# Weight conversions of the first block in halves, and some copies moved between ScalarE and VectorE

## The chip, the cores and the metric

The kernel runs on one NeuronCore of a Trainium2 chip. Its metric is the device time of one execution in microseconds (us). The core has five engines that run in parallel, each through its own list of instructions in order: TensorE (PE, matrix products into PSUM), VectorE (DVE), ScalarE (ACT), GpSimd (POOL) and SyncE (SP, which here only issues transfers). An instruction waits on semaphores until what it reads is written and what it overwrites is no longer needed; whatever stands behind it on the same engine waits with it.

## What is computed

The reference, cut to what matters:

```python
# x: (8, 3008, 256), filt_r and filt_i: (1505, 256), w_in: (256, 2048), w_out: (2048, 256)
X = np.fft.rfft(x, axis=1)
Y = X * (filt_r + 1j * filt_i)[None, :, :]
y = np.fft.irfft(Y, n=3008, axis=1).astype(np.float32)

t = y.reshape(8 * 3008, 256)
h = t @ w_in
g = h * np.clip(h + 3.0, 0.0, 6.0) / 6.0
out = g @ w_out                          # float32
```

First a filter along the sequence in the frequency domain, for each of 8 batches; then a two-layer network with a hard swish on each of the 24064 tokens. The two weight matrices come in as 64-bit floats (their scale factor makes them so), which the kernel reads as pairs of 32-bit words and converts itself.

## The kernel before

**Tiling.** The tokens are cut into 47 blocks of 512. A block takes 8 steps (`NP`), one for each 256 columns of the hidden layer: an up-projection (two products of 512 columns in `al` and `be` of PSUM), the hard swish, and in the next step the down-projection, which accumulates in `po`. Blocks from 1 on do this with seven products in place of eight (Strassen's scheme, `up_1` to `up_5`, `g_sums`, `down`), with sums of weight tiles that GpSimd makes once (`w_sums`, L296). Block 0 does it plainly (`plain_up` L653, `plain_down` L662), because the sums don't exist yet.

**The filter.** The Fourier transforms are matrix products in two stages over 3008 = 47 x 64. For batch 0 they run ahead of block 0: `a0_unit` (L348) does the first stage, four products for each half of the channels, and evicts each bank of PSUM with `copy`, on VectorE or ScalarE (L344, L346); `turn` transposes; `b_unit`, `f_unit` and `y_unit` do the second stage and the product with the filter; `bi_unit` and `direct`/`n_first` the way back. Small dummy products (`keep_warm`, L778) are put between. For batches 1 to 7 the same work is spread over the steps of the blocks before they are needed. Of batch 1, `a_unit` (L378) runs once in each of steps 2 to 9, its eight parts `c` in order; both halves of its result are evicted on ScalarE (L388) and stored to DRAM by `z_store`. Later batches evict one half there, and `a_sums` (L392) forms sum and difference on VectorE.

**The weights.** They are 16 parts, part 2p being the 256 columns of the first matrix that step p needs and part 2p + 1 the 256 rows of the second. `w_load` brings a part into a buffer that is borrowed from another pool (`W_AT` names which; a new load waits until the part before the last in the same pool is converted, `w_before`). `w_abs` (L263) makes the absolute value of the high words on ScalarE. `w_conv` (L269) then does the conversion with seven VectorE instructions, L275 to L293; without `w_abs` there is an eighth, L284. The space of `w_all` that the last parts fill holds batch 0's x before.

**Order.** Nothing reorders the work: instructions go to each engine as the Python code emits them. Ahead of block 0 the code is written out (L741 to L830): loads on SP in order, part 0 loaded after the third piece of x, part 1 after the fourth; a conversion after `a0_unit(4)` and after `a0_unit(16)`; parts 2 and 3 converted after the second stage, by `convert(2)` at L830. From then on a plan says what is added to each step: `at(step, fn, ...)`. Functions in `EARLY` (L732) are emitted between up- and down-projection, others at the end of the step. In block 0, step p emits `plain_up(p)`, the early part, `plain_down(p - 1)`, the late part. `plain_up` also emits the two rectifiers on ScalarE (`relu`, L616) and the two gate products on VectorE (`hswish`, L621), which release `al` and `be`. Twelve conversions stand in the late part of steps 0 to 6:

```python
for i, s in enumerate((0, 1, 1, 2, 2, 3, 3, 4, 4, 5, 5, 6)):
    at(s, convert_one)
```

`convert_one` emits `w_abs`, `w_conv` and then whatever loads have their buffer free. The GpSimd sums for weight part i follow from step 6 on, parts 14 and 15 first.

The functions that the change touches, with the line numbers of the profile:

Of the kernel before, what the change touches and what calls it, by code (L numbers as in the profile page):

```python
# [36 lines left out]
HC = NC // 2  # L37
XC = 4
NB = HC // XC
# [6 lines left out]
NP = DFF // 256  # L46
# [90 lines left out]
def kernel(  # L137
# [9 lines left out]
    nc = tc.nc  # L147
# [47 lines left out]
    st = {}  # L195
# [38 lines left out]
    def w_part(i):  # L234
        p = i // 2
        if i % 2 == 0:
            cols = ts(p, 256)
            src = moe_w_in[:, cols].bitcast(I32)
            return src.rearrange("(a p) d -> p a d", p=P), w_in[p][:, 0:4, :].rearrange("p (a j) m -> p a (j m)", a=2)
        src = moe_w_out[ts(p, 2 * P), :].bitcast(I32)  # L240
        return src.rearrange("(a p) d -> p a d", p=P), w_out[p][:, 0:4, :].rearrange("p (a j) m -> p a (j m)", a=2)
# [21 lines left out]
    def w_abs(i):  # L263
        words = st["bits", i].rearrange("p (n two) -> p n two", two=2)
        st["high", i] = sp.tile([P, 512], FP32, name="s1")
        nc.scalar.activation(out=st["high", i], in_=words[:, :, 1].bitcast(FP32), func=AXT.Abs)


    def w_conv(i):  # L269
        words = st.pop(("bits", i)).rearrange("p (n two) -> p n two", two=2)  # L270
        lo, hi = words[:, :, 0], words[:, :, 1]
        big, rest = (yp.tile([P, 2, D], FP32, name="y").bitcast(I32).rearrange("p a n -> p (a n)") for j in range(2))
        v = nc.vector
        high = st.pop(("high", i), None)
        v.tensor_scalar(out=big, in0=hi, scalar1=3, scalar2=0x3FFFFFFF,  # L275
                        op0=ALU.logical_shift_left, op1=ALU.bitwise_and)
        v.scalar_tensor_tensor(out=big, in0=hi, scalar=top_c, in1=big,  # L277
                               op0=ALU.bitwise_and, op1=ALU.bitwise_or)
        v.tensor_scalar(out=rest, in0=big, scalar1=23, scalar2=23,
                        op0=ALU.logical_shift_right, op1=ALU.logical_shift_left)  # L280
        v.tensor_scalar(out=lo, in0=lo, scalar1=9, scalar2=0x3F800000,
                        op0=ALU.logical_shift_right, op1=ALU.bitwise_or)
        if high is None:
            v.tensor_scalar(out=hi, in0=hi, scalar1=1, scalar2=1,  # L284
                            op0=ALU.logical_shift_left, op1=ALU.logical_shift_right)
            high = hi.bitcast(FP32)
        rest, big = rest.bitcast(FP32), big.bitcast(FP32)
        v.scalar_tensor_tensor(out=rest, in0=lo.bitcast(FP32), scalar=1.0, in1=rest,  # L288
                               op0=ALU.subtract, op1=ALU.mult)
        v.scalar_tensor_tensor(out=rest, in0=rest, scalar=2.0 ** -20, in1=big, op0=ALU.mult, op1=ALU.add)  # L290

        two = lambda t: t.rearrange("p (a d) -> p a d", a=2)
        v.scalar_tensor_tensor(out=w_part(i)[1], in0=two(high), scalar=1.125 * 2.0 ** -15, in1=two(rest),  # L293
                               op0=ALU.is_ge, op1=ALU.mult)
# [44 lines left out]
    def zt(dh):  # L339
        return (xn.rearrange("p a n -> p (a n)"), xs.rearrange("p i j d -> p (i j d)"))[dh]  # L340

    def copy(dve, to, ps):
        if dve:
            nc.vector.tensor_copy(out=to, in_=ps)  # L344
        else:
            nc.scalar.activation(out=to, in_=ps, func=AXT.Copy)  # L346

    def a0_unit(j):  # L348
        for dh in range(2):
            ps = bank(0)  # L350
            for u in range(4):
                nc.tensor.matmul(ps[:, ts(u, P)], x0[0:64 + NA, j + u, ts(dh, P)], st["start"][0:64 + NA, ts(1, P)],  # L352
                                 start=True, stop=True)
            copy(dh and j < 8, zt(dh).rearrange("p (n j) -> p j n", j=HC)[:, j:j + 4, :],
                 ps.rearrange("p (j n) -> p j n", j=4)[:, :, 0:4 * KH])

    def turn(c):
# [11 lines left out]
    def bank(b):  # L369
        if b:  # L370
            return psF.tile([P, 512], FP32, name="psf", tag="f")
        st["bank"] = i = (st.get("bank", -1) + 1) % 4
        return psO.tile([P, 2, 2, P], FP32, name="po%d" % i).rearrange("p a u m -> p (a u m)")
# [4 lines left out]
    def a_unit(b, c):  # L378
        xc = xs[:, (b * NB + c) % 3, :, :]
        t = t1p.tile([P, XC // 2, 2, D], FP32, name="t1")  # L380
        ps = [bank(b).rearrange("p (j d) -> p j d", d=D) for h in range(2)]
        for j in range(2):
            for g in range(2):
                for h in range(2):
                    nc.tensor.matmul(ps[h][ts(g, 64), j, :], wa[ds(h * 64, NA), ds((c * XC + 2 * g + j) * 2 * KH, 64)],  # L385
                                     xc[ds(h * 64, NA), 2 * g + j, :], start=True, stop=True)
        for h in range(2 if b == 1 else 1):
            nc.scalar.activation(out=t[:, :, h, :], in_=ps[h], func=AXT.Copy)  # L388
        st["t1", b, c] = t, ps[1]


    def a_sums(b, c):  # L392
        t, ps = st["t1", b, c]
        nc.vector.tensor_tensor(out=t[:, :, 1, :], in0=t[:, :, 0, :], in1=ps, op=ALU.subtract)
        nc.vector.tensor_tensor(out=t[:, :, 0, :], in0=t[:, :, 0, :], in1=ps, op=ALU.add)  # L395

# [100 lines left out]
    for b in range(B):  # L497
        j = 0
        while j < HC:
            n = 1 if b == 0 and j == NJ else min(NJ, HC - j)  # L500
# [229 lines left out]


    EARLY = (a_unit, b_unit, bi_unit, n_unit)  # L732

    def at(step, fn, *a):
        plan.setdefault((step, fn in EARLY), []).append((fn, a))

    with tc.manual_schedule():
# [22 lines left out]
        def convert(n):  # L760
            nonlocal done
            for i in range(n):
                w_conv(done)
                done += 1


        def convert_one():
            nonlocal done
            w_abs(done)
            w_conv(done)  # L770
            done += 1
            load_bits(NCONV)

# [2 lines left out]
        ps = psU.tile([P, 512], FP32, name="al")  # L776
# [3 lines left out]
                nc.tensor.matmul(ps, zero[:, P:2 * P], zero, start=True, stop=True)  # L780

        keep_warm(2)
        for j, n, bits in (0, 4, 0), (4, 4, 0), (8, 8, 1), (16, 8, 2), (24, 4, 2), (28, 4, 2):
            x0_load(j, n)
            load_bits(bits)
        table_load(0, 0)
# [2 lines left out]
        for j in range(0, HC, 4):  # L789
            a0_unit(j)  # L790
            keep_warm({4: 2, 12: 2, 20: 1}.get(j, 0))
            convert(j in (4, 16))
        nc.gpsimd.memset(t4, 0.0)
        for c in range(FB, NT):
            table_load(0, c)
# [19 lines left out]
            if c == 4:  # L815
                t4_load(0, 0, KH - 3 * TC, 1)
        t4_load(0, KH - 3 * TC, KH - TC, 1)
        for i in 2, 3:
            w_abs(i)
        direct(NU - 2)  # L820
        direct(NU - 1)
# [5 lines left out]
        for c in range(2):  # L827
            x_load(1, c)
            load_bits(7 + c)
        convert(2)  # L830

        def wai_load():
            nc.sync.dma_start(wa[:, 528:], wa_d[:, 528:])
# [2 lines left out]
        at(0, bi_unit, 0, NU - 2)  # L836
        at(0, g_store, 0, NU - 2)

        for i, s in enumerate((0, 1, 1, 2, 2, 3, 3, 4, 4, 5, 5, 6)):
            at(s, convert_one)  # L840

        for i in range(2):
            at(6, w_sums, 2 * NP - 2 + i, False)
        for p in range(NP):
            for i in range(2):
                if p < NP - 1:
                    at(p + 6, w_sums, 2 * p + i, False)
                at(p + 6, w_sums, 2 * p + i, True)

        at(0, wai_load)  # L850
        at(2, x_load, 1, 2)
# [42 lines left out]
        for n in range(1, B):  # L894
            a_at, f_at, y_at, bi_at = places(n)
            for c, s in enumerate(a_at):
                at(s, a_unit, n, c)
                if n > 1:
                    at(s, a_sums, n, c)
                at(s, z_store, n, c, nc.sync if n == 1 else nc.gpsimd)  # L900
                if c >= 3:
                    at(max(a_at[c - 3], s - 6), x_load, n, c)
                elif n > 1:
                    at(max(prev[c + NB - 3], s - 6), x_load, n, c)
            for c in range(NT):
                s = f_at[2 * (c - TB) + (n == 1)] + 1 if c >= TB else a_at[-1] + 1
                at(s, t2_load, n, c)
                s = f_at[2 * (c - FB) + 1] + 1 if c >= FB else a_at[-1 if n > 1 else 3] + 1
                at(s, table_load, n, c)
            for i in range(NU):  # L910
                if i % 2 == 0 or n == 1:
                    at(f_at[i], b_unit, n, i)
                if i % 2 == 0:
                    at(bi_at[i // 2], bi_unit, n, i)
                    at(bi_at[i // 2], g_store, n, i)
                at(y_at[i], y_unit, n, i)
            for i in range(NU):
                at(f_at[i], f_unit, n, i)
            prev = a_at
# [4 lines left out]
        for i in range(len(items) + 1):  # L924
            up = i < len(items)
            k, p = items[min(i, len(items) - 1)]
# [54 lines left out]
        k, v, add = NBLK - 1, nc.vector.tensor_tensor, ALU.add  # L981
# [37 lines left out]
```

## Time and profile before

| | |
|---|---|
| median of 8 runs | 2701.54 us (2700.47 to 2704.62) |
| profiled execution | 2700.95 us |
| its span, first to last instruction | 2699.2 us |
| TensorE, matmul | 2675.5 us busy, 99% of the span |
| VectorE | 2017.5 us, 75% |
| ScalarE | 1309.4 us, 49% |
| GpSimd | 365.6 us, 14% |
| mean granted TensorE clock | 0.998 |

"Busy" is the time in which an engine executes; for the matmuls the end is modelled, so that a busy TensorE is not one at its peak. Rows of the timeline give the start and the length of an instruction (or of a run of equal ones), the engine, the line of the kernel, the operation, output and inputs by tile, and in brackets the idle time before it with what ended it. Rows of the windows give a stretch, its length, the busy time of PE, PEld (weight loads), DVE, ACT and POOL in it, the granted clock, the share of the DMA engines and GB/s. In "PE al L658 <- DVE g L621: 3.0, 3, 1.3" the instructions of line 658 on PE waited for those of line 621 on DVE for 3.0 us in total, 3 times, at most 1.3 us.

### The profile page before, as it was taken

The page shows a single profiled execution, that of the slowest core. Times are in us where ns is not written, and L with a number is a line of the kernel's source. Part 1 is how long each engine was busy: PE and PEld are TensorE (multiplying, and loading weights), DVE is VectorE, ACT ScalarE, POOL GpSimd, SP SyncE. Part 2 cuts the span into 40 slices and gives each one's busy share as a digit, 9 for nine tenths or more (in the row PEclk, how much of TensorE's full clock was granted, in tenths as well). Part 3 has the DMA queues.
Part 4 walks back from the last instruction along what each step waited for, and adds up shares of the span by engine and source line. Part 5 has one row for each costly group of instructions (what it writes and reads, how often), then busy time and mean ns, then how long its engine had stood idle before and what let it go on. Part 6 is the DMA issues. An engine that isn't in the chain of part 4 may idle for free.

```text
span 2699.2 us, 48892 instructions
## 1 busy us (share of the span) xinstructions
PE 2675.5 (99%) x18846; PEld 2368.3 (88%) x18846; DVE 2017.5 (75%) x3500; ACT 1309.4 (49%) x2617; POOL 365.6 (14%) x598
## 2 busy tenths in 40 slices
PE   9999999999999999999999999999999999999998
PEld 6588898888988888888888888988888888899997
DVE  7868867787678776787767877677776778766665
ACT  4444444445444444454544545445444454445443
POOL 2141011001210012101121011211112111000000
PEclk9999999999999999999999999999999999999999
DMA  8732133211332113311133111331123321110000
GB/s 237 218 95 70 47 89 100 68 35 42 92 99 63 36 47 95 99 55 37 47 97 96 55 39 53 89 96 55 39 55 90 93 60 35 42 31 18 18 9 17
DMA packets 106598, 185.89 MB, mean 69 GB/s; under 512 B 23609, under 2 KB 66297, under 8 KB 106049
## 3 DMA queue, kind: packets, MB, share of 16 engines
q1 hardware_dynamic: 88607, 138.05, 18.2%
q0 software_dynamic: 17152, 44.22, 6.2%
q8 instruction: 149, 2.44, 0.4%
q14 instruction: 84, 0.69, 0.1%
q10 hardware_dynamic: 606, 0.49, 0.1%
HBM read 110.74 MB, written 71.93 MB: 68 GB/s over the span
## 4 chain that ended last, share of the span: by engine, by line
PE 96%; DVE 2%; DMA 0%; ACT 0%; issue 0%; POOL 0%; POOLq 0%; DVEq 0%; SPq 0%
PE po L647 43%; PE al L571 24%; PE be L571 18%; PE psn L525 4%; PE psf L472 2%; PE psf L385 2%; PE psf L428 1%; PE po L352 1%; PE po L437 0%; PE psf L437 0%; DVE g L621 0%; DVE y L277 0%; DVE y L288 0%; PE al L780 0%; DVE w_all L293 0%; DVE y L290 0%
## 5 line engine op out<-in xcount | busy, mean ns | idle before, releaser
L647 PEld LDWEIGHTS po<-w_all,g 128*128 128x128 f32 x10304 | 1364.3, 192 | 148.3 <-issue 41.4
L647 PE MATMUL po<-w_all,g 128*128 128x128 f32 x10304 | 1403.8, 277 | 0.6 <-DVE g L621 0.6
L616 ACT ACTIVATE r<-h,half_c 128x512 f32<-128x512 f32 x736 | 531.1, 722 | 328.5 <-DVE h L597 316.4
L621 DVE SCALAR_TENSOR_TENSOR g<-r,h 128x512 f32<-128x512 f32 x736 | 508.2, 690 | 206.3 <-ACT r L616 191.5
L571 PE MATMUL al<-xt,w_all 128*128 128x256 f32 x2208 | 660.6, 381 | 1.1 <-DVE h L602 0.6
L571 PE MATMUL be<-xn,w_all 128*128 128x256 f32 x1472 | 438.1, 379 | 0.0
L597 DVE TENSOR_TENSOR h<-be,s 128x512 f32<-128x512 f32 x368 | 254.3, 691 | 219.7 <-PE be L571 208.4
L571 PEld LDWEIGHTS al<-xt,w_all 128*128 128x128 f32 x2208 | 335.6, 192 | 2.5 <-DVE h L602 1.2
L571 PEld LDWEIGHTS be<-xn,w_all 128*128 128x128 f32 x1472 | 280.2, 190 | 37.5
L611 ACT ACTIVATE h<-al 128x256 f32<-128x256 f32 x368 | 141.0, 383 | 344.3 <-PE al L571 344.3
L602 DVE TENSOR_TENSOR h<-al,s 128x256 f32<-128x256 f32 x368 | 156.3, 425 | 167.1 <-PE al L571 166.0
L629 DVE TENSOR_TENSOR g<-g 128x512 f32<-128x512 f32 x368 | 256.0, 696 | 12.6
L592 ACT ACTIVATE s<-al 128x256 f32<-128x256 f32 x368 | 141.3, 384 | 206.0 <-PE al L571 204.0
L583 ACT ACTIVATE s<-be 128x256 f32<-128x256 f32 x368 | 141.1, 383 | 176.6 <-PE be L571 176.6
L571 PE MATMUL al<-xn,w_all 128*128 128x256 f32 x736 | 220.1, 381 | 0.5 <-ACT h L611 0.5
L571 PE MATMUL be<-xt,w_all 128*128 128x256 f32 x736 | 219.1, 379 | 0.0
L631 DVE TENSOR_TENSOR g<-g 128x256 f32<-128x256 f32 x368 | 170.0, 462 | 12.5
L582 ACT ACTIVATE s<-al 128x256 f32<-128x256 f32 x368 | 141.0, 383 | 71.4 <-PE al L571 71.3
L628 DVE TENSOR_TENSOR g<-g 128x256 f32<-128x256 f32 x368 | 157.2, 427 | 12.6
L571 PEld LDWEIGHTS be<-xt,w_all 128*128 128x128 f32 x736 | 140.1, 190 | 18.7
L402 POOL DMA_DIRECT2D z_tmp<-t x192 | 95.2, 502 | 417.3 <-DVE t L395 399.0
L492 POOL DMA_DIRECT2D g_tmp<-t x84 | 52.7, 632 | 584.6 <-ACT t L475 584.6
(139 smaller groups left out, 1813.1 us busy)
## 6 DMA issues: line engine op xcount, KB each, us to landing
g_tmp<-t POOLq DMA_DIRECT2D x96, 256.0 KB, 3.7
t<-g_tmp SPq DMA_DIRECT2D x188, 120.0 KB
t<-z_tmp SPq DMA_DIRECT2D x42, 512.0 KB
z_tmp<-t POOLq DMA_DIRECT2D x192, 96.0 KB, 3.5
out_dram<-o SPq DMA_DIRECT2D x321, 47.0 KB
xs<-in_x_dram SPq DMA_DIRECT2D x112, 128.0 KB
ft<-in_filt_r_dram SPq DMA_DIRECT2D x168, 64.0 KB
ft<-in_filt_i_dram SPq DMA_DIRECT2D x168, 64.0 KB
```

The lines of the kernel that those rows point to most:

```text
L571: nc.tensor.matmul(ps, w_in[p][:, w, :], x, start=start, stop=stop, skip_group_check=True)
L582: nc.scalar.activation(out=s[:, 0, :], in_=al, func=AXT.Copy)
L583: nc.scalar.activation(out=s5, in_=be[:, 1, :], func=AXT.Copy)
L592: nc.scalar.activation(out=s[:, 1, :], in_=al, func=AXT.Copy)
L597: nc.vector.tensor_tensor(out=st["h"][0].rearrange("p (a n) -> p a n", a=2), in0=be, in1=s, op=ALU.add)
L602: nc.vector.tensor_tensor(out=st["h"][1][:, 256:512], in0=al, in1=s5, op=ALU.add)
L616: nc.scalar.activation(out=r, in_=st["h"][i], func=AXT.Relu, bias=half_c, scale=1.0 / 6.0)
L621: nc.vector.scalar_tensor_tensor(out=st["g", k, p][:, o:o + 2, :].rearrange("p a n -> p (a n)"), in0=st["r", i], scalar=1.0, in1=st["h"][i ...
L628: v.tensor_tensor(out=g[:, G1, :], in0=g[:, G3, :], in1=g[:, G22, :], op=ALU.add)
L629: v.tensor_tensor(out=g[:, G3:G2 + 1:2, :], in0=g[:, G3:G1 + 1, :], in1=g[:, G11:G11 + 1, :].broadcast_to([P, 2, 256]), op=ALU.subtract)
L631: v.tensor_tensor(out=g[:, G4, :], in0=g[:, G12, :], in1=g[:, G2, :], op=ALU.subtract)
L647: nc.tensor.matmul(st["po", k][bank][:, part, u, :], g[:, a, ts(u, P)], w_out[p][:, w, :], start=(p == 0 and n in OPENS and u == 0), stop= ...
```

## The change

- `w_conv` is cut in two: the first four VectorE instructions stay, the rest become `w_conv_2`.
- In the steps of block 0 the conversions are emitted by halves, 3 in each of steps 0 to 5, 4 in step 6 and 2 in step 7; the loads are looked at after each second half.
- Part 1 is loaded after the first filter table rather than among x, and converted with parts 2 and 3 ahead of block 0, not in the first stage. `w_abs` is now done for parts 1, 2 and 3.
- In `a0_unit` the second copy goes to VectorE for all j but 8 and 12; before for j = 0 and 4 alone.
- In parts 6 and 7 of batch 1's first stage, the second eviction goes to VectorE, in `a_sums`.
- GpSimd's sums for part 15 move from the front to where the part stands in order.

```diff
@@ w_conv
-        high = st.pop(("high", i), None)
+        st["conv", i] = big, rest, lo, hi
...
         v.tensor_scalar(out=lo, in0=lo, scalar1=9, scalar2=0x3F800000,
                         op0=ALU.logical_shift_right, op1=ALU.bitwise_or)
+
+    def w_conv_2(i):
+        big, rest, lo, hi = st.pop(("conv", i))
+        v = nc.vector
+        high = st.pop(("high", i), None)
@@ a0_unit
-            copy(dh and j < 8, zt(dh).rearrange("p (n j) -> p j n", j=HC)[:, j:j + 4, :],
+            copy(dh and j not in (8, 12), zt(dh).rearrange("p (n j) -> p j n", j=HC)[:, j:j + 4, :],
@@ a_unit
-        for h in range(2 if b == 1 else 1):
+        for h in range(2 if b == 1 and c < NB - 2 else 1):
@@ a_sums
+        if b == 1:
+            if c >= NB - 2:
+                nc.vector.tensor_copy(out=t[:, :, 1, :], in_=ps)
+            return
@@ convert
                 w_conv(done)
+                w_conv_2(done)
@@
-        def convert_one():
+        def convert_half(second):
             nonlocal done
-            w_abs(done)
-            w_conv(done)
+            if not second:
+                w_abs(done)
+                w_conv(done)
+                return
+            w_conv_2(done)
             done += 1
             load_bits(NCONV)
@@
-        for j, n, bits in (0, 4, 0), (4, 4, 0), (8, 8, 1), (16, 8, 2), (24, 4, 2), (28, 4, 2):
+        for j, n, bits in (0, 4, 0), (4, 4, 0), (8, 8, 1), (16, 8, 1), (24, 4, 1), (28, 4, 1):
@@
-            convert(j in (4, 16))
+            convert(j == 4)
@@
-        for i in 2, 3:
+        for i in 1, 2:
             w_abs(i)
@@
-        convert(2)
+        w_abs(3)
+        convert(3)
@@
-        for i, s in enumerate((0, 1, 1, 2, 2, 3, 3, 4, 4, 5, 5, 6)):
-            at(s, convert_one)
-
-        for i in range(2):
-            at(6, w_sums, 2 * NP - 2 + i, False)
-        for p in range(NP):
-            for i in range(2):
-                if p < NP - 1:
-                    at(p + 6, w_sums, 2 * p + i, False)
-                at(p + 6, w_sums, 2 * p + i, True)
+        half = 0
+        for s, n in enumerate((3, 3, 3, 3, 3, 3, 4, 2)):
+            for i in range(n):
+                at(s, convert_half, half % 2)
+                half += 1
+
+        order = [2 * NP - 2] + [i for i in range(2 * NP) if i != 2 * NP - 2]
+        for i in order:
+            at((6 + i // 2) if i != order[0] else 6, w_sums, i, False)
+            if i != order[0]:
+                at(6 + i // 2, w_sums, i, True)
+        at(6 + NP - 1, w_sums, order[0], True)
@@
-                if n > 1:
-                    at(s, a_sums, n, c)
+                at(s, a_sums, n, c)
```

## The prediction

> **What bounds the kernel now.** I read the page's busy line first, then the windows of the first 300 us by tens, then PE's waits in the one stage that the change touches (70 to 145 us), then its timeline. The busy line says where a microsecond counts:
>
> ```profile
> PE 2675.5 (99%) x18846; PEld 2368.3 (88%) x18846; DVE 2017.5 (75%) x3500; ACT 1309.4 (49%) x2617; POOL 365.6 (14%) x598
> ```
>
> TensorE is busy for the whole span, so work moved off another engine gains nothing unless TensorE waits for it, and a delay of TensorE anywhere is carried to the end. The waits of TensorE between 70 and 145 us, in total, times, longest:
>
> ```profile
> PE al L658 <- DVE g L621: 3.0, 3, 1.3
> PE al L571 <- ACT s L592: 0.5, 1, 0.5
> PE al L571 <- ACT h L611: 0.5, 1, 0.5
> ```
>
> So in the first block, where VectorE converts the weights, TensorE loses 3.0 us to it, and 0.5 us to ScalarE in the step after. The windows (PE, PEld, DVE, ACT, POOL, clock, DMA) show both sides: VectorE is full to 130 us, and has room at 60 to 70 and after 130.
>
> ```profile
> 60.00:70.00 10.00, 8.45 (x44) 5.81 (x43) 5.93 (x10) 1.96 (x5) 1.13 (x2) 1.00 0.82 254
> 100.00:110.00 10.00, 9.34 (x50) 5.99 (x49) 9.55 (x16) 2.92 (x6) 2.51 (x3) 1.00 0.31 92
> 120.00:130.00 10.00, 8.74 (x42) 5.08 (x41) 9.42 (x17) 3.94 (x7) 1.55 (x3) 1.00 0.77 211
> 130.00:140.00 10.00, 9.46 (x64) 6.54 (x63) 3.52 (x7) 4.06 (x9) 7.44 (x17) 1.00 0.59 160
> ```
>
> The timeline gives the durations (start, length, engine, line):
>
> ```profile
> 70.17 0.69 DVE L621 SCALAR_TENSOR_TENSOR g<-r,al 128x512 f32<-128x512 f32 x1 [3.86 <-ACT r L616]
> 71.89 0.69 DVE L621 SCALAR_TENSOR_TENSOR g<-r,be 128x512 f32<-128x512 f32 x1 [1.03 <-ACT r L616]
> ...
> 77.86 0.42 DVE L275 TENSOR_SCALAR y<-xt 128x512 int32<-128x512 int32 x1
> 79.91 0.69 DVE L288 SCALAR_TENSOR_TENSOR y<-xt,y 128x512 f32<-128x512 f32 x1
> 81.44 0.69 DVE L293 SCALAR_TENSOR_TENSOR w_all<-s,y 128x512 f32<-128x512 f32 x1
> 82.05 0.42 DVE L275 TENSOR_SCALAR y<-bits 128x512 int32<-128x512 int32 x1
> ...
> 117.29 1.99 PE L658 MATMUL al<-xn,w_all 128*128 128x512 f32 x4 [1.17 <-DVE g L621]
> 126.93 1.98 PE L658 MATMUL al<-xn,w_all 128*128 128x512 f32 x4 [1.26 <-DVE g L621]
> ```
>
> A conversion takes 4.19 us of VectorE (77.86 to 82.05): 2.05 for the first half, 2.14 for the second. A gate product (L621) takes 0.60 to the next instruction. From an up-projection's first matmul (67.43) the first product can start 2.74 us later (70.17), the second 4.46 later (71.89): two matmul groups of 1.72, an eviction each. TensorE starts 0.74 after the VectorE instruction it waits for (product at 116.55, matmul at 117.29).
>
> **The change, part by part.** I write U5 for the up-projection of step 5.
>
> *First stage.* The load of part 1 moves behind x and table 0, its conversion behind parts of the second stage, and four copies go from ScalarE to VectorE. From 6.67 to 25.60 us the chain is TensorE alone, and TensorE's order is unchanged: earlier x gains nothing. ScalarE's copies took 0.84 to 0.90 each at one per 0.89 us of matmul; the last starts at 25.60, and on VectorE (0.83) it ends at the same time. 0.
>
> *Conversions 1 to 3 in a row.* They start at 57.88 and end at 57.88 + 3 x 4.17 = 70.4, where two ended at 66.3. The cover is VectorE's idle 3.86 us before 70.17; the first product is 0.2 late, the second waits for U0 until 71.89 anyway. 0.
>
> *Order in the block.* Before, conversions per step are 1, 2, 2, 2, 2, 2, 1, 0; after, in halves, 3, 3, 3, 3, 3, 3, 4, 2. Up(p) needs part 2p. Before, part 12 was converted in step 4 and part 14 in step 5, a full step ahead. Now part 12's second half is the last thing VectorE does in step 5 and part 14's the last in step 6, so U6 and U7 wait for a conversion that ends immediately ahead of them, while the products of step 6 and 7, which come next on VectorE in order, wait for U6 and U7. What ran side by side becomes one chain. Step by step, with TensorE's own time between ups from the trace (8.2 us from U2 to U3, 9.9 from U3 to U4 and from U4 to U5, 8.3 from U5 on, stalls taken out):
> - U2: the product of step 1 comes after half of part 5, at 78.65, so U2 starts at 79.4 (79.07 before).
> - U3 at 87.5, U4 at 97.4, both by TensorE (87.18, 97.09).
> - U5: products of step 4 at 101.4, then part 10: 102.5 + 4.19, and the GpSimd subtractions (L564) that fall on it. These stretched part 10 by 1.35 us before (5.54 from 101.47 to 107.01). Its last instruction starts at 107.6, U5 at 108.3 (107.75).
> - Step 5: second product at 108.3 + 4.46 = 112.8, VectorE idle 1 to 2 us on the way. Then 11b, 12a, 12b: 113.4 + 2.14 + 2.05 + 1.53 = 119.1, U6 at 119.9 (117.29). TensorE was ready at 116.5: it stalls 3.45 us.
> - Step 6: second product at 124.3, then 13 and 14: 124.9 + 4.19 + 3.58 = 132.7, U7 at 133.4 (126.93). TensorE was ready at 128.0: it stalls 5.5 us.
> - Step 8 starts 8.1 after U7, 6.5 us later than before. The same sum for the kernel before gives U5, U6 and U7 at 107.8, 117.3 and 126.9. Without GpSimd's stretch it is 5.4, with 2.0 of stretch 7.2; I take 6.5.
>
> *Loads.* The loads of parts 12 to 15 wait on SP for conversions 10 to 13, ahead of z stores and x loads behind them. Part 12's must land before 115.4: issued at about 108 (behind an x load that goes ahead of it now), and such a load took 4.3 us to ScalarE's absolute value (105.63 to 109.97). The x loads are used a step or more later. 0.
>
> *GpSimd.* Its weight sums wait for part 14, so from 133; those of part 0 need two groups of three at 0.57 before step 8 at 141. 0. They also lie on part 15's conversion, which ends at 142.7 without them and is needed at 145: 2.4 us of cover against a stretch that was 1.35 on part 10; without cover, at most 1 us. 0.
>
> *Two first-stage copies of batch 1 to VectorE.* In step 8, ScalarE's two evictions (L388, 137.72 to 138.69) hold back the eviction (L592) that TensorE waits for in that step: the 0.5 us row above. One less gives 0.45. In step 9 L592 starts 0.03 after its matmul: 0. The copies themselves (0.69) fall in VectorE idle of 3.5 and 1.3 us.
>
> *The clock.* The trace shows what TensorE's clock does after idling (last matmul ends at 2687.83), and over a short gap:
>
> ```profile
> 63.00:64.00 1.00, 0.00 (x0) 0.00 (x0) 0.96 (x3) 0.00 (x0) 0.00 (x0) 1.00 0.93 283
> ...
> 2689.00:2690.00 1.00, 0.00 (x0) 0.00 (x0) 0.93 (x4) 0.00 (x0) 0.19 (x1) 1.00 0.00 0
> 2690.00:2691.00 1.00, 0.00 (x0) 0.00 (x0) 0.32 (x1) 0.00 (x0) 1.00 (x3) 0.53 0.23 61
> ```
>
> A gap of 1.2 us left it at full; 2.2 us after the last matmul it fell to 0.50. The price of a cold start is in the first stage: four passes of 512 columns took 3.78 us at 2.89 and 1.88 at 10.38, 1.9 us lost (though the clock's column shows 1.00 there). New gaps of 3.45 and 5.5 us lie beyond 2.2, so by the rows each costs a cold start, on the path both times: 3.8. Bounds: 0 (no drop), and 2.4 each if the first copy stage's slow 4.08 us (3.57 later) is counted too.
>
> The Trainium skill, "TensorE: Matmul & The Clock Gate", Part 1, says that an idle window of about 3.4 us halves the clock, and that about 3.4 us of work brings it back. This speaks against a change that opens gaps. The trace halves it sooner (2.2 us). By the page, an estimate, the gap of 3.45 us would cost nothing and the one of 5.5 about 1.7, so +7.8 in place of +9.8.
>
> **Sum.** 6.5 - 0.45 + 3.8 = +9.8 us. The profiled execution took 2700.95 us (span 2699.2, 1.75 around it), 0.6 below the median of 2701.54. 2701.54 + 9.8 = 2711.3 us.
>
> **Rivals.**
> 1. *Same chain, no or one cold start.* The windows around 63 show that short gaps are free. +6.1 with none (2707.6), +8.0 with one (2709.5).
> 2. *VectorE leads after all, and the change is faster.* For it: the products of steps 2 to 4 come up to 5.5 us earlier (101.4 for 107.01). If part 12 were done before TensorE is ready (116.5), the three stalls of 3.0 us and 0.45 would go: 2698.1. Against: by U6 VectorE has done the same nine conversions and twelve products as before, which took until 117.75 without a pause.
> 3. *The chain is shorter.* If GpSimd doesn't touch part 10 and no clock falls, 5.4 - 0.45 = +4.9, 2706.4; this is within 0.2% (5.4 us, about what a measurement of this kernel can tell from no change).
> 4. *More is lost.* Part 15 stretched beyond its cover (+1) and two cold starts of 2.4: 2713.5.
>
> **How the numbers follow.** Forecast, two cold starts: 0.45. Rival 1: 0.33, nearly all over 0.2%. Rival 3: 0.08. Rival 4: 0.09. Rival 2: 0.05. The range of 8 in 10 leaves out rival 2, rival 3 in part and the worst of rival 4: 2706.0 to 2713.6. Of the forecast alone: 2709.8 to 2712.6. Faster 0.05, within 0.2% 0.09, slower 0.86.
>
> **What would show it.** Right: TensorE's waits at the up-projection name the conversion's last instruction, two long ones, 3.5 and 5.5 us, before U6 and U7; VectorE shows idle before products of steps 5 to 7, ended by ScalarE; a clock under 1.00 around 120 and 133; step 8 starts at 141 to 146. Wrong: U6 before 118, or gaps with a full clock, or TensorE waiting for the loads of parts 12 to 15 or for GpSimd's sums.

## The result, and the profile after

The changed kernel took 2711.25 us (median of 10 runs, 2709.84 to 2715.53) where the kernel before took 2701.42 (28 runs beside it): a ratio of 1.0036, with a 95% interval of 1.0028 to 1.0044. It is 9.8 us slower; the forecast was 2711.3. The profiled execution has a span of 2709.6 us against 2699.2, and a mean granted clock of 0.996 against 0.998.

The busy line of the kernel after:

```profile
PE 2680.1 (99%) x18846; PEld 2368.0 (87%) x18846; DVE 2022.9 (75%) x3505; ACT 1306.9 (48%) x2612; POOL 367.5 (14%) x598
```

TensorE has the same 18846 instructions, and is busy 4.6 us longer with them: nearly half the loss is no wait at all, but slower matmuls. The rest is mostly in the waits of TensorE between 70 and 152 us (in total, times, longest):

```profile
PE al L667 <- DVE w_all L298: 9.0, 3, 5.3
```

Before, the up-projection waited 3.0 us for the gate product `g`; now it waits 9.0 us for the last instruction of a weight conversion. Of the two waits of 0.5 us for ScalarE in step 8, one is gone and the other, at 154.96, now lies behind this window. The windows by tens (PE, PEld, DVE, ACT, POOL, clock, DMA share, GB/s):

```profile
100.00:110.00 10.00, 9.23 (x50) 5.97 (x49) 9.55 (x15) 3.85 (x7) 2.73 (x3) 1.00 0.36 103
110.00:120.00 10.00, 6.95 (x39) 4.20 (x37) 7.68 (x14) 3.03 (x5) 0.00 (x0) 1.00 0.48 148
120.00:130.00 10.00, 10.00 (x40) 5.44 (x40) 4.45 (x8) 3.60 (x6) 0.00 (x0) 0.83 0.58 170
130.00:140.00 10.00, 4.71 (x7) 2.11 (x7) 4.96 (x10) 0.69 (x1) 4.14 (x10) 0.70 0.73 184
140.00:150.00 10.00, 9.87 (x62) 6.29 (x62) 6.12 (x10) 4.08 (x8) 9.37 (x18) 0.96 0.35 93
```

Up to 110 us the windows show little that is new. From there both engines are idle in turns: VectorE, full to 130 us before, is at 7.7, 4.5 and 5.0 of ten, and TensorE at 7.0, 10.0 and 4.7. That is one chain through two engines. The clock, 1.00 before, is 0.83 and 0.70 from 120 to 140 us, and 0.96 in the last window. TensorE's timeline shows the three up-projections (start, length, engine, line, and in brackets the idle time before):

```profile
108.52 1.98 PE L667 MATMUL al<-xn,w_all 128*128 128x512 f32 x4 [0.69 <-DVE w_all L298]
110.34 1.88 PE L667 MATMUL be<-xn,w_all 128*128 128x512 f32 x4
119.95 3.52 PE L667 MATMUL al<-xn,w_all 128*128 128x512 f32 x4 [3.05 <-DVE w_all L298]
123.26 2.08 PE L667 MATMUL be<-xn,w_all 128*128 128x512 f32 x4
135.31 3.78 PE L667 MATMUL al<-xn,w_all 128*128 128x512 f32 x4 [5.29 <-DVE w_all L298]
138.88 2.80 PE L667 MATMUL be<-xn,w_all 128*128 128x512 f32 x4
```

The waits are 0.69, 3.05 and 5.29 us, ahead of U5, U6 and U7. From the first matmul to the end of the second group U5 takes 112.22 - 108.52 = 3.70 us, U6 5.39, U7 6.37: 1.69 and 2.67 us of slower matmuls, 4.36 together. VectorE's timeline shows the link that closes the chain:

```profile
119.20 0.69 DVE L298 SCALAR_TENSOR_TENSOR w_all<-s,y 128x512 f32<-128x512 f32 x1
124.23 0.69 DVE L630 SCALAR_TENSOR_TENSOR g<-r,al 128x512 f32<-128x512 f32 x1 [4.33 <-ACT r L625]
126.10 0.69 DVE L630 SCALAR_TENSOR_TENSOR g<-r,be 128x512 f32<-128x512 f32 x1 [1.19 <-ACT r L625]
126.71 0.43 DVE L275 TENSOR_SCALAR y<-bits 128x512 int32<-128x512 int32 x1
...
134.56 0.69 DVE L298 SCALAR_TENSOR_TENSOR w_all<-s,y 128x512 f32<-128x512 f32 x1 [0.20 <-DMA bits<-in_moe_w_out_dram]
```

Part 12 is done at 119.2 + 0.69, and U6 starts at 119.95. VectorE then has nothing it may do for 4.33 us: the next instruction in its order is the product of U6, which ScalarE has to rectify first. Part 14, which U7 needs, stands behind the two products and part 13, and U7 starts 0.75 after part 14's last instruction does.

From U1 to the first product of step 8 it took 63.06 us before (72.08 to 135.14) and 73.79 after (72.40 to 146.19): +10.7, of which 6.0 is longer waits (9.0 for 3.0) and 4.4 slow matmuls; the remaining 0.3 is nearly all U2, which starts 7.24 us after U1 for 6.99. Everything else of the kernel lies outside this stretch, and the spans differ by 10.4.

### The profile page after: what moved, and what is told of

Same layout as the page of the kernel before. It is cut to its first block, busy times and chain, and to the rows that moved or that the text cites. A ratio compares the mean times of both kernels' runs of the same rounds, so it can differ in the third digit from the quotient of the medians.

```text
span 2709.6 us, 48886 instructions
## 1 busy us (share of the span) xinstructions
PE 2680.1 (99%) x18846; PEld 2368.0 (87%) x18846; DVE 2022.9 (75%) x3505; ACT 1306.9 (48%) x2612; POOL 367.5 (14%) x598
## 4 chain that ended last, share of the span: by engine, by line
PE 96%; DVE 3%; issue 0%; ACT 0%; DMA 0%; POOL 0%; POOLq 0%; SPq 0%; DVEq 0%
PE po L656 43%; PE al L580 24%; PE be L580 18%; PE psn L534 4%; PE psf L481 2%; PE psf L390 2%; PE psf L437 1%; PE po L357 1%; PE al L667 0%; PE psf L446 0%; PE po L446 0%; DVE y L277 0%; DVE g L630 0%; PE al L793 0%; DVE w_all L298 0%; PE be L667 0%
```

## The experiments

Each experiment undoes or changes one thing. Two measures are given: the time, and "the block", the distance from U1's first matmul to the first product of step 8 in the profiled execution, 63.06 before and 73.79 after. My theory: the order of the halves makes a chain of TensorE, ScalarE and VectorE, some 6 us longer than the old order, and the gaps that it leaves cost two starts at half clock. Rivals: the changed first stage, loads or copies cost the time; or the chain alone does, and the clock is not in it.

### The order of the halves alone

```diff
-        for s, n in enumerate((3, 3, 3, 3, 3, 3, 4, 2)):
+        for s, n in enumerate((2, 4, 4, 4, 4, 4, 2, 0)):
```

> The changed kernel with one line undone: 2, 4, 4, 4, 4, 4, 2, 0 halves per step, which puts each conversion back into the step it had before; parts of the first stage, the copies and the order of GpSimd's sums stay changed. If the wait of U6 and U7 on the conversion that ends just ahead of them makes the loss (my theory), both gaps go, the clock stays at 1.00, and the time is that of the kernel before less 0.4 us for the copies: 2701.0, between 2699.5 and 2702.5. If the first stage's move, the copies or the sums carry a part of the loss, that part stays: 2704 or more. If cutting a conversion in two costs by itself, nothing differs from that here either, since the halves now follow each other directly.

Measured: 2700.64 us (2700.04 to 2704.05), ratio to before 1.0001 (0.9992 to 1.0011), the block 63.02. TensorE's waits in this kernel:

```profile
PE al L667 <- DVE g L630: 3.0, 3, 1.3
```

This has everything of the change but the place of the halves, and the whole loss is gone; even the three old stalls are back, of the old length and behind the gate product. The loads, the first stage, the copies and GpSimd's order cost nothing together that the block shows (63.02 for 63.06); the times alone, by their interval, could hide some 3 us.

### The gaps filled with work

Small products are put ahead of U6 and U7, so that TensorE doesn't idle while it waits.

```diff
+                if up and p > 5:
+                    fill = psU.tile([P, 512], FP32, name="al")
+                    for _ in range((3, 6)[p - 6]):
+                        nc.tensor.matmul(fill, w_in[0][:, 0, :], xb(0, 0), start=True, stop=True)
```

> The changed kernel with TensorE kept busy in its two gaps: 3 dummy products of 128x512 ahead of U6 and 6 ahead of U7, into al, whose result nothing reads (0.86 us each at full clock, in gaps of 3.05 and 5.29 us). The conversions and waits stay as they are. If the cold starts cost what the trace shows (1.7 us and 2.7 us more for the up-projection after each gap), the clock stays at 1.00 and the time falls by 4.4 us to 2706.9, between 2706 and 2708. If the clock's fall costs nothing on the path, because VectorE sets the pace there, the time stays at 2711 or rises a little with the dummy products.

Measured: 2707.21 us (2706.3 to 2710.64), ratio 1.0024 (1.0015 to 1.0033), the block 69.54. Its timeline of TensorE, the added products (L952) and what follows them:

```profile
116.66 2.74 PE L952 MATMUL al<-xn,w_all 128*128 128x512 f32 x6
119.96 1.96 PE L667 MATMUL al<-xn,w_all 128*128 128x512 f32 x4 [0.57 <-DVE w_all L298]
...
128.15 5.31 PE L952 MATMUL al<-xn,w_all 128*128 128x512 f32 x12
133.68 1.96 PE L667 MATMUL al<-xn,w_all 128*128 128x512 f32 x4 [0.22 <-DVE w_all L298]
```

And its windows:

```profile
120.00:130.00 10.00, 10.00 (x45) 5.94 (x46) 6.02 (x11) 3.61 (x6) 0.00 (x0) 1.00 0.67 186
130.00:140.00 10.00, 9.78 (x41) 4.67 (x40) 5.77 (x10) 2.95 (x5) 5.78 (x13) 1.00 0.64 193
```

More work on TensorE made the kernel faster by 4.0 us. U6 starts where it did (119.96 for 119.95), since VectorE sets its start; but its four passes take 1.96 for 3.52, the clock stays at 1.00, and with the products of step 6 earlier U7 comes 1.6 us sooner. So the slow clock costs 4.0 by the times, 73.79 - 69.54 = 4.25 by the block. What is left against before, 69.54 - 63.06 = 6.5, is the chain without the clock.

### The two copies of batch 1 alone, in the kernel before

```diff
-        for h in range(2 if b == 1 else 1):
+        for h in range(2 if b == 1 and c < NB - 2 else 1):
...
+        if b == 1:
+            if c >= NB - 2:
+                nc.vector.tensor_copy(out=t[:, :, 1, :], in_=ps)
+            return
...
-                if n > 1:
-                    at(s, a_sums, n, c)
+                at(s, a_sums, n, c)
```

> The kernel before with one part of the change alone: in parts 6 and 7 of batch 1's first stage the second eviction goes to VectorE. My theory: 0.4 us less in step 8, where ScalarE's two evictions hold back the one TensorE waits for, so 2701.0 against 2701.4, too small to be told by the times and to be read in the trace from step 8's length (9.17 us before). Rival: VectorE's copy delays the gate product behind it, and the step is as long or longer.

Measured: 2700.43 us (2699.45 to 2700.83), ratio 0.9995 (0.9986 to 1.0005); the block 63.05. The waits of TensorE keep their 3.0 us in the block and lose one of the two rows of 0.5 in step 8:

```profile
PE al L662 <- DVE g L625: 3.0, 3, 1.3
PE al L575 <- ACT h L615: 0.5, 1, 0.5
```

Step 8 is 0.4 us shorter (8.77 for 9.17, from its first product to that of step 9), as the sum had it. The times can't tell a gain of 0.4 from none.

### The first stage undone, the halves kept

Part 1's load and conversion and the four copies in `a0_unit` are put back; the block keeps its 3, 3, 3, 3, 3, 3, 4, 2.

```diff
-            copy(dh and j not in (8, 12), zt(dh).rearrange("p (n j) -> p j n", j=HC)[:, j:j + 4, :],
+            copy(dh and j < 8, zt(dh).rearrange("p (n j) -> p j n", j=HC)[:, j:j + 4, :],
...
-        for j, n, bits in (0, 4, 0), (4, 4, 0), (8, 8, 1), (16, 8, 1), (24, 4, 1), (28, 4, 1):
+        for j, n, bits in (0, 4, 0), (4, 4, 0), (8, 8, 1), (16, 8, 2), (24, 4, 2), (28, 4, 2):
...
-            convert(j == 4)
+            convert(j in (4, 16))
...
-        for i in 1, 2:
+        for i in 2, 3:
...
-        w_abs(3)
-        convert(3)
+        convert(2)
```

> The changed kernel with its first stage undone: part 1 loaded among x and converted there, two conversions ahead of the block, the first-stage copies as before. The block keeps its 3, 3, 3, 3, 3, 3, 4, 2 halves. My theory: the move of part 1 and the copies are neither cost nor gain, since TensorE alone is on the path there and VectorE's idle time takes the third conversion; the two gaps stay and the time stays at 2711, between 2710 and 2712.5. Rival: the third conversion ahead of the block makes VectorE late and feeds the gaps, and a part of the 10 us goes with it: 2709 or less.

Measured: 2710.7 us (2710.05 to 2711.39), ratio 1.0035 (1.0022 to 1.0048), the block 73.37, and TensorE's wait is that of the changed kernel to the tenth:

```profile
PE al L667 <- DVE w_all L298: 9.0, 3, 5.3
```

With the first experiment this settles the place: without the changed first stage the loss stays, and with the old order of the halves it goes. (The two copies of batch 1 and GpSimd's order were not undone together with the first stage; the first experiment has them both, and no loss.)

### Four more halves in step 5

```diff
-        for s, n in enumerate((3, 3, 3, 3, 3, 3, 4, 2)):
+        for s, n in enumerate((3, 3, 3, 3, 3, 7, 2, 0)):
```

> The changed kernel with 3, 3, 3, 3, 3, 7, 2, 0 halves: parts 13 and 14 are converted in step 5, in front of the gate products of step 6, not behind them, so that U7 doesn't wait for them in one chain with U6. U6 still waits for part 12. My theory: the gap before U6 stays with its cold start, the one before U7 goes; U7 at about 129.9 and step 8 at 138.0 in place of 146.2, so 2703.0, between 2702 and 2705. Rival: what counts is how late VectorE runs as a whole; then four halves moved ahead of the products delay these by 8.4 us, U7 with them, and the time stays at 2710 or more.

Measured: 2703.62 us (2702.25 to 2709.56), ratio 1.0012 (1.0003 to 1.0021), the block 65.56. TensorE's waits and U6 to U7 of this kernel:

```profile
PE al L667 <- DVE w_all L298: 3.7, 2, 3.1
```

```profile
123.96 3.21 PE L667 MATMUL al<-xn,w_all 128*128 128x512 f32 x4 [3.05 <-DVE w_all L298]
126.97 2.40 PE L667 MATMUL be<-xn,w_all 128*128 128x512 f32 x4
133.87 1.88 PE L667 MATMUL al<-xn,w_all 128*128 128x512 f32 x4
```

Part 14 is converted in step 5 again, and U7 follows the down-projection with no wait; U6 still waits its 3.05 us, because part 12 is where it was. The two gaps are two separate prices. (In this profiled execution U1 starts 4.0 us later than in the changed kernel, 76.42 for 72.40, at half clock behind a wait of 1.74 us for a load. That lies outside the block; the profiled run took 2707.24 us, and eight of the ten took 3 to 5 us less.) Taken from U1, U7 and step 8 come at 57.45 and 65.56 us, where the forecast's 129.9 and 138.0 are 57.5 and 65.6 behind the changed kernel's U1.

### One conversion more ahead of the block

In the kernel before VectorE is busy for 5.9 of the ten us from 60 to 70, and has little room from there to 130. Here part 1 is loaded and converted in the first stage as before, and parts 2, 3 and 4 ahead of the block, so that it has eleven conversions and not twelve; the halves are spread by when a part is needed.

```diff
-            copy(dh and j not in (8, 12), zt(dh).rearrange("p (n j) -> p j n", j=HC)[:, j:j + 4, :],
+            copy(dh and j < 8, zt(dh).rearrange("p (n j) -> p j n", j=HC)[:, j:j + 4, :],
...
-        for j, n, bits in (0, 4, 0), (4, 4, 0), (8, 8, 1), (16, 8, 1), (24, 4, 1), (28, 4, 1):
+        for j, n, bits in (0, 4, 0), (4, 4, 0), (8, 8, 1), (16, 8, 2), (24, 4, 2), (28, 4, 2):
...
-            convert(j == 4)
+            convert(j in (4, 16))
...
-        for i in 1, 2:
+        for i in 2, 3:
...
-        w_abs(3)
+        w_abs(4)
...
-        for s, n in enumerate((3, 3, 3, 3, 3, 3, 4, 2)):
+        for s, n in enumerate((3, 3, 3, 4, 4, 3, 2, 0)):
```

> A mixture: part 1 is loaded and converted in the first stage as before, parts 2, 3 and 4 are converted ahead of the block, where the kernel before left VectorE idle for 3.9 us, and the remaining 22 halves stand 3, 3, 3, 4, 4, 3, 2, 0 per step, so that no part ends just ahead of its use; the copies of batch 1 stay changed, those of the first stage are as before. My theory says that a conversion less in the block takes VectorE off the path: the three stalls of TensorE before U5, U6 and U7 (3.0 us) go but for 0.5 at U2, and 0.4 for the copies: 2701.4 - 2.5 - 0.4 = 2698.5, between 2697.5 and 2700. Rival: part 4's load lands too late for the idle time (it is issued at 61 us), VectorE waits for it, and the time is 2701 or more.

Measured: 2696.76 us (2696.52 to 2700.33), ratio 0.9985 (0.9976 to 0.9995), the block 59.61. It is faster than either kernel, and better than expected, below the whole range. TensorE waits for VectorE nowhere in the block; its windows:

```profile
110.00:120.00 10.00, 10.00 (x56) 5.74 (x58) 9.62 (x17) 4.65 (x8) 0.00 (x0) 1.00 0.70 207
120.00:130.00 10.00, 10.00 (x57) 6.36 (x48) 7.93 (x13) 4.26 (x8) 8.40 (x15) 1.00 0.78 215
```

TensorE is busy for all of it, U5 to U7 follow at 8.11 us each, and VectorE has 2 us to spare in the second window. Against before the block is 3.45 shorter, 3.0 of it the stalls behind the gate product. With the 0.4 of step 8 that makes 3.9 of the 4.5 us by the times; the other 0.6 was not traced.

### The same, with the halves as early as before

```diff
-        for s, n in enumerate((3, 3, 3, 4, 4, 3, 2, 0)):
+        for s, n in enumerate((2, 4, 4, 4, 4, 4, 0, 0)):
```

> The mixture of before (part 1 in the first stage, three conversions ahead of the block) with the rest put back into steps by whole conversions, 2, 4, 4, 4, 4, 4, 0, 0 halves. It has a conversion less in the block, but as many ahead of each step's products up to step 5 as the kernel before. My theory: TensorE waits for products, and those of steps 4 and 5 come after as much of VectorE's work as before, so most of the 3.0 us of stalls return: 2700.5, between 2699.3 and 2701.3. Rival: one conversion less is the whole gain, and the time is that of the mixture, 2696.8.

Measured: 2701.56 us (2700.5 to 2704.94), ratio 1.0001 (0.9991 to 1.001), the block 63.85: the whole gain is gone again, and a little more than expected. TensorE's waits:

```profile
PE al L667 <- DVE g L630: 3.8, 3, 2.0
```

The old stalls are back. With the conversions bunched early, the gate products stand behind two full conversions in each step, and TensorE waits for a product to free `al`. So a conversion fewer is worth nothing by itself: the halves must lie late enough to let the gate products through, and early enough for their part. The other way round, all twelve conversions placed by need, was not run, so whether the conversion fewer is needed at all stays open. (As in the experiment on step 5, this profiled execution ran at half clock ahead of U0, behind a wait of 1.65 us, and its 2704.94 us are the longest of the ten.)

### The same, with the halves later still

```diff
-        for s, n in enumerate((3, 3, 3, 4, 4, 3, 2, 0)):
+        for s, n in enumerate((1, 3, 4, 4, 4, 4, 2, 0)):
```

> The mixture with 1, 3, 4, 4, 4, 4, 2, 0 halves, which also keeps the products of step 1 in front of U2 (it waited 0.3 us in the mixture). By my sums TensorE then never waits for VectorE in the block: 0.3 us less than the mixture, 2696.4, which the times can't tell; the trace should show no wait of the up-projections on VectorE, and U2 directly behind the down-projection. Rival: four halves in steps 2 to 5 delay the products of some step, and a wait returns there: 2697.5 or more.

Measured: 2699.77 us (2699.22 to 2700.6), ratio 0.9995 (0.9985 to 1.0004), the block 62.11. This missed by 3.4 us. No up-projection waits for VectorE, which was right; the loss is elsewhere. U4 starts 12.77 us after U3, where it is 9.9 in all other kernels. ScalarE's timeline in that step:

```profile
84.35 0.67 ACT L266 ACTIVATE s<-bits 128x512 f32<-128x512 f32 x1
91.00 0.68 ACT L266 ACTIVATE s<-xt 128x512 f32<-128x512 f32 x1 [5.98 <-DMA xt<-in_moe_w_in_dram]
91.59 0.67 ACT L625 ACTIVATE r<-al,half_c 128x512 f32<-128x512 f32 x1
92.16 0.68 ACT L625 ACTIVATE r<-be,half_c 128x512 f32<-128x512 f32 x1
92.72 0.56 ACT L540 ACTIVATE xn<-psn 128x470 f32<-128x470 f32 x1
```

The absolute value of part 8 waits 5.98 us for its load, and the rectifiers and the eviction L540, which TensorE needs for its next product, wait behind it. TensorE idles 1.26 us, and then the clock falls:

```profile
92.00:93.00 1.00, 0.07 (x1) 0.00 (x0) 0.93 (x4) 1.00 (x3) 0.00 (x0) 1.00 1.06 412
93.00:94.00 1.00, 0.67 (x11) 0.50 (x14) 0.97 (x2) 0.28 (x1) 0.18 (x1) 1.00 1.05 266
94.00:95.00 1.00, 1.00 (x8) 0.56 (x3) 0.90 (x2) 0.54 (x2) 0.99 (x1) 0.74 0.91 264
95.00:96.00 1.00, 1.00 (x4) 0.82 (x3) 1.00 (x2) 1.00 (x4) 0.00 (x0) 0.50 0.76 184
```

The down-projection in this stretch takes 5.41 us instead of 3.72. The load was late because loads are only looked at behind a second half: step 0 has none now, so part 8's was issued a step later. That reading of the miss is what the last run tests.

### The late load mended

```diff
         convert(3)
+        load_bits(NCONV)
```

> The kernel with the halves 1, 3, 4, 4, 4, 4, 2, 0, with one thing added: the loads are looked at once more right behind the conversions ahead of the block, so that part 8's load is issued some 13 us sooner (there it was issued at 84.70, because step 0 holds no second half any more, and landed at 91). If that late load was what made the spread version miss (ScalarE 6.0 us behind it, a gap of 1.3 on TensorE and half a clock in the second stage's way back), ScalarE's wait for xt goes from 6.0 to under 1, TensorE's clock stays at 1.00 through the block, and the time is 2696.4 (2695.5 to 2697.5). If it was the order of the conversions itself, the wait goes but the time stays at 2699 to 2700.

Measured: 2697.03 us (2696.38 to 2700.17), ratio 0.9984 (0.9975 to 0.9994), the block 59.25. The load of part 8 in SP's timeline, with the halves as they were, and here:

```profile
84.70 0.40 SPq L260 DMA_DIRECT2D xt<-in_moe_w_in_dram  x1
```

```profile
71.38 0.40 SPq L260 DMA_DIRECT2D xt<-in_moe_w_in_dram  x1
```

Issued 13.3 us sooner, it is no longer waited for: ScalarE's row of 6.0 us is gone, TensorE has no wait in the block, and 2.7 us are won. So the miss was the load, not the order. This kernel and the one with 3, 3, 3, 4, 4, 3, 2, 0 can't be told apart by their times; both are 4.3 to 4.5 us faster than before and some 14 faster than the change.

## Why the prediction was right

- *The chain, +6.5.* Measured +6.5 (block with the gaps filled, against before). Step by step: U2 at 79.64 for a forecast of 79.4, U3 87.85 for 87.5, U4 97.76 for 97.4, U5 108.52 for 108.3, all with 0.3 us from ahead of the block (U0 starts between 67.07 and 67.96 in the profiles of these kernels, but for the two that ran at half clock ahead of it). U6 at 119.95 for 119.9, a stall of 3.05 for 3.45. U7 at 135.31 for 133.4, because U6's slow start is passed on through the chain, which the sum put down as a price of its own; with the gaps filled U7 starts at 133.68. The stall before it is 5.29 for 5.5.
- *Two cold starts, 3.8.* Right in number; the sizes were 1.7 and 2.7, together 4.4 (4.0 by the times with the gaps filled). The forecast took 1.9 for each, from a row of the first stage where the clock's column shows 1.00; the second lasted longer. Luck has a part in this term: it was counted by the length of the gaps, which is not what decides (the last section), and its price was borrowed from another place. Rival 1, with none or one, falls with the clock's column and with the filled gaps.
- *The page's rule.* By the Trainium skill, "TensorE: Matmul & The Clock Gate", Part 1, the first gap would have cost nothing and the change +7.8, an estimate of the forecast. The gap of 3.05 us, under the page's 3.4, cost 1.7; the rows of this case were the better guide, though not for the reason that the forecast gave.
- *The copies, -0.45.* 0.4, seen in step 8 alone and in the kernel before with the copies alone.
- *The total.* The terms as measured add up to 6.5 + 4.4 - 0.4 = 10.5, as the spans do (10.4); by the medians it is 9.8. That 2711.25 meets 2711.3 to the tenth is luck; a forecast within 1 us is what the working earns.
- *Costed at nothing.* First stage and loads: 0 in the first experiment. The conversions 1 to 3 in a row: the first product of step 0 comes 0.2 late (70.70, 2.95 behind U0), the second in time, as worked out. GpSimd stretched part 10 by 1.5 us (forecast 1.35) and part 15 by 0.9; part 15 was still done at 148.1, 2.3 us before the down-projection that reads it (150.38): hidden. One small thing wasn't in the sum: part 14's last instruction waited 0.20 us for what its row names a transfer, and this lies in U7's chain.
- *Rival 2, faster.* It needed part 12 done before TensorE is ready for it. The trace has it 3 us too late. The experiments show one way to make it true: one conversion fewer in the block, and the halves of the rest placed by need.

## What to carry to other kernels

When pieces of work are spread evenly over steps, compute for each piece when its last instruction ends, and when its consumer is ready; then look at what stands next on the producer's queue. If that is itself work on the consumer's result, the two engines take turns from there on, and both idle. Too early is wrong as well: pieces that are bunched ahead of need delay the short instructions that free the bottleneck's buffers. And a gap on TensorE can have two prices, the wait and a start at half clock behind it (1.7 and 2.7 us here); when work is moved to a later place, see to it that the loads which are issued from that place don't move with it.

## What was not expected of the hardware

The clock doesn't follow the length of the gap alone. These gaps of TensorE were followed by half clock: 1.26 us (the kernel with the late load), 1.65 and 1.74 (ahead of U0, in two profiles), 3.05 and 5.29 (the changed kernel). These were not: 1.26 (ahead of U7 in the kernel before), 1.05 to 1.52 (ahead of U0 in the other kernels), 2.00 (ahead of U7 with the halves bunched). The rule that I took from the end of the kernel, that short gaps leave the clock at full and 2.2 us halve it, held for the gaps it was used on but not for these.

The fall can also come after TensorE has gone back to work. Windows of one microsecond of the changed kernel, those in which the clock changes:

```profile
120.00:121.00 1.00, 1.00 (x2) 0.54 (x3) 0.00 (x0) 0.00 (x0) 0.00 (x0) 0.62 0.84 281
123.00:124.00 1.00, 1.00 (x3) 0.44 (x2) 0.00 (x0) 0.49 (x1) 0.00 (x0) 0.67 0.84 194
133.00:134.00 1.00, 0.00 (x0) 0.00 (x0) 0.97 (x2) 0.00 (x0) 0.00 (x0) 0.95 0.99 342
140.00:141.00 1.00, 1.00 (x2) 0.33 (x2) 0.53 (x1) 0.00 (x0) 1.00 (x3) 0.64 0.52 131
```

U6 restarts at 119.95 with the clock at 1.00. A mean of 0.62 in the next microsecond is full clock for a quarter of it and half for the rest, so the clock falls near 120.24; by the same reading it comes back near 123.66, falls again in the gap near 133.9, and comes back near 140.7: 3.4 and 6.8 us at half clock. The same page, in Part 1, has the clock watched over a window of about 3.4 us that runs free of the program. The traces of this case show such a grid. The three later changes lie 1, 4 and 6 steps of 3.413 us behind the first, and the fall behind the last matmul, at 2700.73 by windows of 0.1 us, lies 756.0 steps behind it; the four other profiles with a fall in the first 150 us fit the same step as well, each with a start of its own. Cut along the grid, the windows of the changed kernel, and below them two of the kernel with the halves bunched:

```profile
116.83:120.24 3.41, 0.36 (x2) 0.29 (x2) 2.86 (x6) 0.00 (x0) 0.00 (x0) 1.00 0.37 116
120.24:123.66 3.42, 3.42 (x5) 1.35 (x5) 0.00 (x0) 0.15 (x1) 0.00 (x0) 0.50 0.86 238
130.48:133.90 3.42, 0.00 (x0) 0.00 (x0) 3.28 (x7) 0.00 (x0) 0.00 (x0) 1.00 0.91 216
133.90:137.31 3.41, 2.00 (x3) 0.97 (x4) 1.15 (x2) 0.00 (x0) 1.77 (x4) 0.50 0.77 217
137.31:140.72 3.41, 3.41 (x6) 1.34 (x5) 0.69 (x1) 0.69 (x1) 3.10 (x9) 0.50 0.57 133
```

```profile
62.97:66.39 3.42, 1.77 (x16) 1.63 (x14) 3.18 (x7) 0.00 (x0) 0.76 (x2) 1.00 0.95 290
127.83:131.24 3.41, 1.78 (x9) 1.22 (x7) 3.24 (x5) 0.00 (x0) 3.25 (x6) 1.00 0.85 246
```

In these profiles half clock lasts whole windows, and it follows a window in which TensorE idled long. The gap of 5.29 us fills one window and takes 1.41 us of the next, which stays at half and is followed by another at half. That gives the two sizes: 3.41 / 2 = 1.7 for U6, and (6.83 - 1.41) / 2 = 2.7 for U7. The gap of 2.00 us that cost nothing is split, 1.63 us in the window shown and 0.37 in the next; the 1.65 us ahead of U0 in the same profile lie in one window, and the clock fell behind it. In all eleven profiles, from 60 to 150 us, a window at full clock with 1.65 us of idle or more (1.65, 1.74, 2.68, 2.80, 3.05, 3.41 and 3.41) was followed by half clock, and one with 1.63 or less was not, but for one, the 1.26 us of the kernel with the late load. (Where a profile has no fall in this stretch, the grid is laid back from the fall at its end.) So a gap's price depends on where it lies in the grid, and 3.05 us split evenly between two windows might have cost nothing.

Idle time alone is not the whole rule, as that one window shows. And in the two profiles that ran at half clock ahead of U0, a window without a gap (66.55 to 69.96, 66.39 to 69.80) was followed by half clock once more. All three hold mostly small products (`128x94`, or 47 x 64 of weights); that these count for less is a guess that no run here tests.
